# The written-out loop over the entries of an attention and gated-MLP kernel, with all steps in another program order

## The chip, the cores and the metric

The kernel runs on one core of a Trainium2 chip. The metric is device time in microseconds (us) for one whole execution: 393.02 us before the change, the median of 3 runs (392.91 to 393.31). All times below are in us. PE is the matmul engine (TensorE), PEld its weight loads, DVE the vector engine, ACT the scalar engine, POOL GpSimd, and SP the engine on whose queue nearly all DMAs are issued.

## The reference

For each of 8 batch entries with 8 heads, 576 positions and head width 64, 32 packed queries `p` attend to `k` and `v`; the result serves as keys and values for `q`; the 512-wide rows that come out pass through a gated MLP.

```python
p_packed = sm_attn(p, k, v)              # softmax(0.125 * p k^T) v
out      = sm_attn(q, p_packed, p_packed)
x = out.transpose(0, 2, 1, 3).reshape(B, S, H * D)       # 8 x 576 x 512
h = np.maximum(x @ w_in, 0.0)                            # 1024 wide
u, v = h[..., :512], h[..., 512:]
v_n = (v - mean(v)) / sqrt(var(v) + 1e-6)
v_s = einsum('ts,bsd->btd', w_spatial, v_n) + b_spatial[None, :, None]
result = (u * v_s) @ w_out
```

## The kernel before

**Arithmetic.** Each large product is made of operands split into a high and a low part, and three matmuls stand for one: high by high, high by low, low by high. The high part is a cast (on ACT mostly), the low part a subtraction (`rest`, line 82, on DVE or POOL). The spatial product and the product with `w_out` are cut in 2 by 2 blocks and done with seven block products each (`gate_product`, line 800, and `product`, line 991). Their operands are blocks, or sums of blocks, of the gated rows: g11, g12, g21, g22 and T1 to T4 (`block_sum`, line 952, on DVE; `block_hi` 977; `block_lo` 987), and of the weights: A11, A12, A22, S1 to S4. Entry 0 has its own, plainer product while the weights are still being prepared, and it is also there that A22, S1 to S4 are split.

**PSUM.** Matmul results go to four quarters of PSUM; `on(i)` (line 74) hands out quarter i, a tile `ps0` to `ps3` of two halves, once all readers of what stood there are done. So a matmul into a quarter waits for the slowest engine that still reads the quarter's old content. In before the quarters are names q0 to q3, renamed at each entry's end.

**Steps of an entry.** `value` (634) makes the v half of h, in three groups of chunks; ACT takes the relu out of PSUM; DVE and POOL work out mean and inverse deviation; ACT applies them (`norm_act`, 735). `up` (869) makes the u half in four blocks. `gate_product` 1 to 7 and `gate_add`, `gate_mult` (856, 861) make the gated blocks in the tile `u`, `product` makes the result. Between them run the attention of the next entry (its packed result `pp`, line 485, and that result's transpose `ppT`, 503; the mixed columns, copied by `mix_keep`, 602; query maxima, exponentials and sums) and the packed attention of the one after (its maxima, `nmax`).

**Order.** PE, DVE, ACT and POOL each run their instructions in the order in which the program names them: the wrapper `InOrder` (line 35) pins every call, which is why every row of the profile has its line, 43. An instruction that waits holds back all that stands behind it on its engine, and nothing else. SP's DMAs are placed by the framework. Entry 0 is written out, entry 1 too (`b = 1`, 1388), entries 2 to 4 are one loop body (1571), entries 5, 6 and 7 are written out again (1746, 1909, 2066).

Of the kernel before, what the change touches and what calls it, by code (L numbers as in the profile page):

```python
# [22 lines left out]
FH = DF // 2  # L23
# [26 lines left out]
def body(ctx: ExitStack, tc, q, k, v, vt, p, w_in, w_sp, b_sp, w_out, out):  # L50
# [1001 lines left out]

# [22 lines left out]
    load_spatial()  # L1075
    att.pack_scores(by_turns(3, 2))
    conv_v1 = to_f32(w_in_sb[:, 2:4, FH:], raw_v1, two, "vr")
    next(conv_v0)
    next(conv_v0)
    att.pack_max(0)  # L1080
    keep_warm(1, 4)
    att.pack_max(1)
    att.pack_exp(0)
    att.pack_exp(1)
    att.pack_turn(on(0), on(3)())
# [75 lines left out]
    ff.value(1, None, (1,), (1,))
    spatial_hi(2)
    ff.value(1, None, (0,), (2,))
    ff.stats(0, (1,))
    load_q(1)
    spatial_rest(3, on(0))
    ff.relu(1, (0,))
    att.query_tail(1)
    spatial_lo(4)
    ff.inverse(0, (0,))  # L1170
    ff.stats(1, (0,))
    ff.value(1, None, (1,), (2,))
    ff.inverse(0, (1,))
    next(bias)
    spatial_lo(3)
    spatial_rest(2, on(3))
    ff.relu(1, (1,))
    ff.norm(0, (0,))
    ff.inverse(1, (0,))
    conv_u1 = to_f32(w_in_sb[:, 2:4, :FH], raw_u1, one, "p1T")  # L1180
    ff.stats(1, (1,))
    ff.norm_hi(0, (0,))
    ff.value(2, on(0))
    spatial_lo(2)
    ff.norm(0, (1,))
    ff.inverse(1, (1,))
    ff.norm(1, (0,))
    ff.norm_hi(0, (1,))
    ff.gate((0,), "hm", (0,), on(2))
    ff.relu(2)  # L1190
    ff.gate((2,), "hm", (0, 1), on(1))
    tail_diff = tail_difference(pool)
    next(tail_diff)
    ff.norm_hi(1, (0,))
    ff.relu_tail()
    next(conv_u0)
    ff.gate((1,), "hm", (0,), on(3))
    ff.gate((0,), "hm", (1,))
    ff.norm(1, (1,))
    ff.gate((1,), "hm", (1,))  # L1200
    ff.norm_lo(1, (0,), pool)
    ff.gate((0,), "hm", (2,))
    ff.stats(2)
    ff.norm_hi(1, (1,))
    ff.gate((3,), "hm", (0, 1), on(0))
    next(conv_u1)
    ff.norm_lo(1, (1,), dve)
    ff.inverse(2)
    ff.gate((0,), "hm", (3,))
    ff.norm_lo(0, (0,), dve)  # L1210
    next(out01)
    ff.gate((1,), "hm", (2,))
    ff.norm_lo(0, (1,), dve)
    ff.gate((3,), "hm", (2, 3))
    out23 = prepare_out(1, raw23)
    next(out23)
    ff.norm(2)
    next(conv_u0)
    ff.gate((1,), "hm", (3,))
    ff.norm_hi(2)  # L1220
    ff.gate((1,), "l", (0, 1))
    ff.gate((0,), "l", (0, 1))
    ff.tail_hi(act.copy)
    ff.norm_lo(2)
    ff.gate((0,), "l", (2, 3))
    next(tail_diff)
    next(conv_u1)
    ff.gate((1,), "l", (2, 3))
    next(tail_diff)
    ff.gate((1,), "t")  # L1230
    ff.gate((0,), "t")
    ff.gate_keep(1, act)
    ff.gate((3,), "l", (0, 1))
    ff.gate_keep(0, act)
    ff.gate((3,), "l", (2, 3))
    nxt.pack_scores(by_turns(2, 3))
    load_k(2)
# [333 lines left out]
    for b in (2, 3, 4):  # L1571
# [135 lines left out]
        if b + 4 < B:  # L1707
            load_k(b + 4)
# [533 lines left out]
```

## Time and profile before

| what | us |
|---|---|
| median of 3 runs | 393.02 |
| span of the profiled execution, first to last instruction | 391.2 |
| median less this span | 1.8 |
| PE busy | 376.8 |
| DVE busy | 326.5 |
| ACT busy | 280.3 |
| POOL busy | 153.5 |

Busy time is the union of an engine's instructions. An entry in the middle of the kernel takes 43.9 us. Tiles carry the names of the program without their numbers: `ps_t` is any quarter of PSUM, `u` the gated rows or their blocks, `o` a spare block for c1 (the sum of gate products 1 and 2), `g_h` and `g_l` the parts of a block, `t` a part of a T sum, `wout_h` and `wout_l` parts of the last weights, `v_h` and `v_l` of the normalized rows, `a_h`, `a_l` and `m_h`, `m_l` of the attention's weights and mixed columns, `kept` the mixed columns' copy, `vr` the v half.

### The profile page before, as it was taken

To read this page: it belongs to the slowest core of one execution; us is meant where nothing else is said; L and a number is where in the kernel's file an instruction comes from. 1 tells how busy PE (TensorE), PEld (TensorE's weight loads), DVE (VectorE), ACT (ScalarE), POOL (GpSimd) and SP (SyncE) were. 2 spreads that over 40 slices of the span, in tenths; PEclk is the share of its full clock that TensorE was granted. 3 is DMA by queue.
4 is the path that set the end of the run, shared out by engine and by line. 5 is a ranking of instruction groups with operands and counts; after the bars stand their busy time and mean duration, and the time that the engine had idled before them with its cause. 6 is when DMAs were issued, how large, how long until landed. Compare 5 with 4: busy or idle time off the path is not lost.

```text
span 391.2 us, 8947 instructions
## 1 busy us (share of the span) xinstructions
PE 376.8 (96%) x3674; PEld 337.8 (86%) x3674; DVE 326.5 (83%) x502; ACT 280.3 (72%) x494; POOL 153.5 (39%) x190
## 2 busy tenths in 40 slices
PE   6889999999999999999999999999899999999995
PEld 5668978799798898998899898998699889999995
DVE  2898989995799959997799959997599969997784
ACT  3588876978975598766985598666895589558642
POOL 3467647899461040702143040703153043504120
PEclk9899999999999999999999999999999999999999
DMA  7999149630510803045300803033000600002003
GB/s 302 416 391 368 68 137 361 252 111 12 185 69 0 335 29 131 0 164 201 116 10 0 331 34 124 0 122 121 4 1 2 241 3 2 0 34 89 2 0 122
DMA packets 17660, 47.79 MB, mean 122 GB/s; under 512 B 1362, under 2 KB 11602, under 8 KB 14804
## 3 DMA queue, kind: packets, MB, share of 16 engines
q1 hardware_dynamic: 17332, 47.02, 32.3%
q8 instruction: 29, 0.48, 0.5%
q10 hardware_dynamic: 288, 0.21, 0.2%
q14 instruction: 11, 0.09, 0.1%
HBM read 37.79 MB, written 9.44 MB: 121 GB/s over the span
## 4 chain that ended last, share of the span: by engine, by line
PE 77%; DVE 10%; ACT 6%; POOL 3%; DMA 2%; issue 1%; SPq 0%; DVEq 0%; ACTq 0%
PE ps_t L43 77%; DMA kT<-in_k 2%; DVE u L43 2%; DVE o L43 1%; ACT vr L43 1%; DVE bn L43 1%; POOL bits L43 1%; DVE vr L43 1%; DVE sm_t L43 1%; POOL sm_t L43 1%; POOL rstd L43 1%; DVE v_l L43 1%; DVE m_l L43 1%; DVE sm L43 1%; ACT sm_t L43 0%
## 5 line engine op out<-in xcount | busy, mean ns | idle before, releaser
L43 POOL TENSOR_TENSOR u<-o,u 128x576 f32<-128x576 f32 x14 | 24.1, 1722 | 71.1 <-DVE o L43 70.6
L43 PE MATMUL ps_t<-t,wout_h 128*128 128x288 f32 x232 | 50.2, 300 | 0.1
L43 POOL TENSOR_TENSOR rstd<-mv,eps 128x2 f32<-128x2 f32 (+2 forms) x26 | 5.8, 222 | 107.2 <-DVE mv L43 107.2
L43 PE MATMUL ps_t<-wb_h,v_h 128*128 128x288 f32 x144 | 40.7, 300 | 0.5 <-ACT kept L43 0.3
L43 PEld LDWEIGHTS ps_t<-t,wout_h 128*128 128x128 f32 x232 | 37.8, 188 | 3.0 <-DVE t L43 2.4
L43 PE MATMUL ps_t<-wb_l,v_h 128*128 128x288 f32 x144 | 39.9, 295 | 0.0
L43 PE MATMUL ps_t<-a_h,m_h 128*128 128x288 f32 x128 | 38.6, 301 | 1.1 <-ACT ppT L43 1.1
L43 DVE TENSOR_TENSOR v_l<-vr,v_h 128x512 fp32r<-128x512 f32 x45 | 31.7, 727 | 7.9 <-ACT v_h L43 7.9
L43 PE MATMUL ps_t<-a_l,m_h 128*128 128x288 f32 x128 | 37.8, 295 | 0.0
L43 PE MATMUL ps_t<-a_h,m_l 128*128 128x288 f32 x128 | 37.8, 295 | 0.0
L43 PE MATMUL ps_t<-t,wout_l 128*128 128x288 f32 x116 | 32.4, 295 | 0.0
L43 PEld LDWEIGHTS ps_t<-wb_h,v_h 128*128 128x128 f32 x144 | 27.0, 188 | 5.1 <-issue 1.4
L43 PE MATMUL ps_t<-g_h,wout_h 128*128 128x288 f32 x104 | 29.2, 296 | 0.9 <-ACT pp L43 0.9
L43 PE MATMUL ps_t<-wsums,v_h 128*128 128x288 f32 x168 | 29.3, 296 | 0.0
L43 PE MATMUL ps_t<-g_h,wout_l 128*128 128x288 f32 x104 | 29.1, 295 | 0.0
L43 ACT CAST v_h<-vr 128x512 fp32r<-128x512 f32 x46 | 27.3, 624 | 2.3 <-DVE vr L43 1.6
L43 PE MATMUL ps_t<-wb_h,v_l 128*128 128x288 f32 x144 | 28.5, 294 | 0.0
L43 PEld LDWEIGHTS ps_t<-wb_l,v_h 128*128 128x128 f32 x144 | 27.1, 188 | 0.0
L43 PE MATMUL ps_t<-m_h,a_h 128*128 128x512 f32 x80 | 26.0, 392 | 0.1
L43 PEld LDWEIGHTS ps_t<-a_h,m_h 128*128 128x128 f32 x128 | 24.0, 188 | 2.3 <-ACT ppT L43 1.3
L43 DVE BATCH_NORM_STATS2 bn<-vr 128x6 f32<-128x512 f32 x32 | 21.1, 681 | 5.7 <-ACT vr L43 5.7
L43 PE MATMUL ps_t<-m_l,a_h 128*128 128x512 f32 x80 | 25.9, 390 | 0.0
(178 smaller groups left out, 1188.4 us busy)
## 6 DMA issues: line engine op xcount, KB each, us to landing
v_sb<-in_v SPq DMA_DIRECT2D x8, 1024.0 KB, 6.6
kT<-in_k SPq DMA_DIRECT2D x7, 1152.0 KB, 5.1
qT<-in_q SPq DMA_DIRECT2D x7, 1152.0 KB, 5.1
out_t<-prod SPq DMA_DIRECT2D x27, 288.0 KB, 2.4
raw<-in_w_in SPq DMA_DIRECT2D x4, 1024.0 KB, 9.4
raw<-in_w_out SPq DMA_DIRECT2D x2, 1024.0 KB, 7.9
kT<-in_k SPq DMA_DIRECT2D x2, 576.0 KB, 7.1
qT<-in_q SPq DMA_DIRECT2D x2, 576.0 KB, 12.4
```

The costliest lines, as they stand in the source:

```text
L43: return lambda *a, **k: self.tc.keep_in_program_order(call(*a, **k))
```

## The change

The eight entries become objects A0 to A7 (attention) and F0 to F7 (MLP), the loop over entries 2 to 4 goes, every step is a call of its own, and quarters are plain numbers. The steps, their engines and the number of instructions are the same; the order in which the calls stand is another nearly everywhere, and entries 2 to 4 no longer have one common order. The queue of SP changes little. Cut to the places that are spoken of:

```diff
-    att, nxt, far, further = (Attention(b) for b in range(4))
+    A0, A1, A2, A3, A4, A5, A6, A7 = (Attention(b) for b in range(B))
     keep_warm(1, 11)
...
     keep_warm(1, 4)
-    att.pack_max(1)
-    att.pack_exp(0)
-    att.pack_exp(1)
-    att.pack_turn(on(0), on(3)())
+    A0.pack_scores(by_turns(3, 2))
...
     out_lo(A12, pool)
...
+    F0.block_lo("g12", pool)
+    out_lo(A22, pool)
+    A1.query_sub(0, pool)
+    A3.pack_scores(by_turns(1, 2))
...
+    A2.pack_values(on(3))
...
+    A1.mix(0, on(0))
...
+    A2.packed(act)
...
+    F0.product(A11, "g11", psum=on(3), to="o11")
...
-    sum_out(S4, dve)
-    out_lo(A22, pool)
...
-    for b in (2, 3, 4):
-        att, nxt, far = nxt, far, further
-        further = Attention(b + 3)
-        ff = FeedForward(b, att, nxt)
...
-    b = 5
...
-    ff.value(0, psum=on(q1), rs=(0,))
-    ff.value(2, psum=on(q0), rs=(0,))
-    ff.value(0, rs=(1,))
-    ff.value(2, rs=(1,))
...
+    F5.value(0, psum=on(0), rs=(0,))
+    F5.value(0, rs=(1,))
+    F5.value(2, psum=on(1), rs=(0,))
+    F5.relu(0)
+    F5.value(2, rs=(1,))
...
+    F5.up_relu(1)
+    A6.packed_turned(act)
...
+    F5.norm_act(1)
...
+    F6.block_hi("g21")
+    F6.block_lo("g21")
+    F6.block_sum("T3")
+    F6.block_sum("T1")
+    F6.block_hi("T3")
```

Three places in the order follow. The number behind a name tells tiles of one name apart and differs between the kernels.

ACT's instructions at the end of entry 0, before: `m_h` is the mixed columns' high part, `a21` a block of the weights, `sm_t` the exponentials of entry 1's queries, `nmax` entry 3's packed maxima, `pp` the packed result of entry 2, read out of quarter 3.

```order
L43 CAST m_h_839<-ps0_t_841 128x1024
L43 CAST g_h_894<-u_577 128x576
L43 CAST a21_898<-bits_631 128x512
L43 ACTIVATE sm_t_851<-sm_t_851 128x576
L43 CAST g_h_894<-u_577 128x576
L43 ACTIVATE sm_t_804<-sm_t_804 128x576
L43 ACTIVATE pp_979<-ps3_t_924,rtot_727 128x64 x2
```

The same place after:

```order
L43 CAST g_h_959<-u_575 128x576
L43 CAST m_h_860<-ps0_t_862 128x1024
L43 CAST g_h_959<-u_575 128x576
L43 ACTIVATE pp_978<-ps3_t_918,rtot_734 128x64 x2
L43 ACTIVATE nmax_894<-nmax_894 128x1
L43 ACTIVATE sm_t_826<-sm_t_826 128x576
L43 ACTIVATE sm_t_807<-sm_t_807 128x576
```

The two rows of `pp` have moved ahead of both exponentials and of the cast of `a21`. On POOL, meanwhile, the low part of A22 (128x512) has moved from after the product into the row between g12's low part (`t`) and the subtraction `sm_t`, both of which stand ahead of g11's low part.

ACT's instructions in entry 5 between the relu of the value group 1 and `ppT`, before:

```order
L43 ACTIVATE vr_3552<-ps3_t_3514 128x1024
L43 COPY p1T_3572<-ps2_t_3538 128x2x4x128
L43 ACTIVATE vr_3510<-vr_3510,off_3576,rstd_3512 128x512 x2
L43 COPY p1T_3572<-ps1_t_3499 128x128
L43 CAST v_h_3489<-vr_3510 128x512
L43 ACTIVATE vr_tail_3527<-vr_tail_3527,off_3601,rstd_3529 64x512
L43 ACTIVATE vr_3552<-vr_3552,off_3611,rstd_3554 128x512 x2
L43 ACTIVATE u_3642<-ps0_t_3559 128x576
L43 COPY ppT_3645<-ps1_t_3499 128x128
```

The same place after:

```order
L43 ACTIVATE vr_3563<-ps3_t_3526 128x1024
L43 COPY p1T_3574<-ps2_t_3539 128x2x4x128
L43 ACTIVATE vr_3507<-vr_3507,off_3571,rstd_3509 128x512 x2
L43 ACTIVATE vr_tail_3513<-vr_tail_3513,off_3583,rstd_3515 64x512
L43 ACTIVATE u_3587<-ps0_t_3550 128x576
L43 COPY p1T_3574<-ps1_t_3504 128x128
L43 ACTIVATE u_3587<-ps3_t_3590 128x576
L43 COPY ppT_3604<-ps1_t_3504 128x128
```

The cast `v_h` and the two halves of `norm_act(1)` no longer stand ahead of `ppT`; the relu of a second block of u now does.

DVE's instructions in entry 6 at the end of the gating, before; `o` here is T3 (the difference g22 less g12), the second `u` is T1, `t` a low part of T3:

```order
L43 TENSOR_TENSOR u_4132<-ps3_t_4234,u_4132 128x2x288
L43 TENSOR_TENSOR o_4270<-u_4132 128x576
L43 TENSOR_TENSOR g_l_4318<-u_4132,g_h_4317 128x576
L43 TENSOR_TENSOR u_4132<-u_4132 128x2x288
L43 TENSOR_TENSOR t_4414<-o_4270,t_4414 128x576
```

The same place after:

```order
L43 TENSOR_TENSOR u_4134<-ps3_t_4232,u_4134 128x2x288
L43 TENSOR_TENSOR g_l_4318<-u_4134,g_h_4317 128x576
L43 TENSOR_TENSOR o_4248<-u_4134 128x576
L43 TENSOR_TENSOR u_4134<-u_4134 128x2x288
L43 TENSOR_TENSOR t_4402<-o_4248,t_4402 128x576
```

The low part of g21 and the sum T3 have changed places.

Two smaller moves are not shown by rows. In entry 1 the cast of v's S3 block on ACT stood before the two copies `kept` of the mixed columns and stands behind them after. In entries 1 to 4 one of the two packed maxima (`pack_most`, a reduction on DVE) stands one place or more earlier among the low parts of v, before the gate's additions.

## Rows read from the trace of the kernel before

**Rows 1.** Part 1 of the page: busy time (share of the span), instructions.
```profile
PE 376.8 (96%) x3674; PEld 337.8 (86%) x3674; DVE 326.5 (83%) x502; ACT 280.3 (72%) x494; POOL 153.5 (39%) x190
```
**Rows 2.** Busy time by stage (columns in the first line; clock 1.00 is full).
```profile
core 0: us, PE busy (x) PEld busy (x) DVE busy (x) ACT busy (x) POOL busy (x), PEclk, DMA share, GB/s
...
168.10:212.00 43.90, 43.90 (x446) 40.48 (x446) 38.06 (x62) 32.93 (x61) 12.20 (x18) 1.00 0.30 109
...
255.90:300.10 44.20, 43.10 (x416) 39.37 (x415) 37.61 (x61) 32.39 (x55) 13.40 (x18) 1.00 0.16 55
```
**Rows 3.** PE in time: start, duration, instruction, in brackets the idle before.
```profile
70.64 1.09 PE L43 MATMUL ps_t<-w_in_sb,ppT 64*32 64x512 f32 x16
72.61 0.40 PE L43 MATMUL ps_t<-g_h,wout_h 128*128 128x288 f32 x1 [0.88 <-ACT pp L43]
...
104.32 0.40 PE L43 MATMUL ps_t<-wb_h,v_h 128*128 128x288 f32 x1 [0.33 <-ACT kept L43]
...
122.01 0.53 PE L43 MATMUL ps_t<-g_l,wout_h 128*128 128x288 f32 x2 [0.49 <-DVE g_l L43]
...
277.08 0.40 PE L43 MATMUL ps_t<-a_h,m_h 128*128 128x288 f32 x1 [1.09 <-ACT ppT L43]
277.32 0.30 PE L43 MATMUL ps_t<-a_l,m_h 128*128 128x288 f32 x1
...
299.66 0.29 PE L43 MATMUL ps_t<-t,wout_h 128*128 128x288 f32 x1
299.79 0.29 PE L43 MATMUL ps_t<-t,wout_l 128*128 128x288 f32 x1
300.09 0.67 PE L43 MATMUL ps_t<-t,wout_h 128*128 128x288 f32 x3
...
339.95 0.53 PE L43 MATMUL ps_t<-g_l,wout_h 128*128 128x288 f32 x2 [0.63 <-DVE g_l L43]
```
**Rows 4.** The chain of waits, 265 to 278 us: start, duration, what.
```profile
267.02 1.04 ACT vr L43
...
274.93 1.41 ACT vr L43 x2
...
276.88 0.16 ACT ppT L43
```
**Rows 5.** POOL and ACT in time before the stall at 72.61 us.
```profile
63.92 2.69 POOL L43 TENSOR_TENSOR wout_l<-bits,wout_h 128x512 fp32r<-128x512 f32 x2 [2.20 <-ACT wout_h L43]
66.57 1.15 POOL L43 TENSOR_TENSOR sm_t<-sm_t,mx 128x576 f32<-128x576 f32 x1
67.69 1.93 POOL L43 TENSOR_TENSOR t<-u,t 128x576 fp32r<-128x576 f32 x1
69.98 1.43 POOL L43 TENSOR_TENSOR g_l<-u,g_h 128x576 fp32r<-128x576 f32 x1 [0.36 <-ACT g_h L43]
...
72.05 0.51 ACT L43 ACTIVATE pp<-ps_t,rtot 128x64 f32<-128x64 f32 x2
```
**Rows 6.** One instruction of POOL and of DVE that start together in entry 1.
```profile
117.92 1.43 POOL L43 TENSOR_TENSOR u<-o,u 128x576 f32<-128x576 f32 x1
...
117.94 2.02 DVE L43 TENSOR_TENSOR u<-o,u 128x576 f32<-128x576 f32 x1
```
**Rows 7.** ACT in time before the stall at 104.32 us.
```profile
99.41 0.63 ACT L43 CAST v_h<-s 128x512 fp32r<-128x512 f32 x1
```
**Rows 8.** DVE in time around the stall at 339.95 us.
```profile
338.47 0.76 DVE L43 TENSOR_TENSOR o<-u 128x576 f32<-128x576 f32 x1
339.14 0.75 DVE L43 TENSOR_TENSOR g_l<-u,g_h 128x576 fp32r<-128x576 f32 x1
...
340.48 0.75 DVE L43 TENSOR_TENSOR t<-o,t 128x576 fp32r<-128x576 f32 x1
```
**Rows 9.** The start and a stretch of entry 5, columns as in rows 2.
```profile
10.00:12.00 2.00, 2.00 (x21) 1.55 (x8) 1.41 (x3) 0.39 (x1) 0.83 (x1) 0.50 1.05 438
...
283.00:288.00 5.00, 5.00 (x38) 5.00 (x39) 4.89 (x8) 4.97 (x9) 0.23 (x1) 1.00 0.00 0
```

More of the change, by code (lines that the diff above doesn't have):

```diff
@@ L1169, in body @@
[L1169 to L1188, printed above, removed]
@@ L1207, in body @@
[L1207 to L1225, printed above, removed]
+    keep_warm(3, 2)
@@ new lines, in body @@
+    A2.query_lo(0)
+    A2.query_hi(1)
+    F1.add_part("P1", A12)
+    A2.query_lo(1)
+    F1.add_part("U", A22)
+    F1.add_part("P3", S1)
+    F1.add_part("P7", S1)
+    load_k(5)
+    load_q(3)
+    A2.query_tail(0, act)
+    A2.query_tail(1, act)
+    F1.put(F1.part("P1"), 0, 0)
+    F1.put(F1.part("P7"), 1, 1)
+    F1.put(F1.part("P3"), 0, 1)
+    F1.put(F1.part("U"), 1, 0)
+    load_v(4)
+    F2 = FeedForward(2, A2, A3)
+    F2.value(0, psum=on(2), rs=(0,))
+    F2.value(0, rs=(1,))
+    F2.value(2, psum=on(0), rs=(0,))
@@ new lines, in body @@
+    A3.query_tail(0, act)
+    A3.query_tail(1, act)
+    F2.product(S1, "T1", onto=S2)
+    F2.add_part("P1", A12)
+    F2.add_part("U", A22)
+    F2.add_part("P3", S1)
+    F2.add_part("P7", S1)
+    load_k(6)
+    F2.put(F2.part("U"), 1, 0)
+    F2.put(F2.part("P3"), 0, 1)
+    load_v(5)
+    load_q(4)
+    F2.put(F2.part("P7"), 1, 1)
+    F2.put(F2.part("P1"), 0, 0)
+    F3 = FeedForward(3, A3, A4)
+    F3.value(0, psum=on(3), rs=(0,))
+    F3.value(0, rs=(1,))
+    F3.value(2, psum=on(2), rs=(0,))
@@ new lines, in body @@
+    A4.query_lo(0)
+    A4.query_turn(1)
+    A4.query_tail(0, act)
+    A4.query_hi(1)
+    F3.add_part("P3", S1)
+    A4.query_lo(1)
+    F3.add_part("P1", A12)
+    F3.add_part("U", A22)
+    F3.add_part("P7", S1)
+    F3.put(F3.part("P1"), 0, 0)
+    load_q(5)
+    F3.put(F3.part("U"), 1, 0)
+    F3.put(F3.part("P3"), 0, 1)
+    load_k(7)
+    F3.put(F3.part("P7"), 1, 1)
+    load_v(6)
+    F4 = FeedForward(4, A4, A5)
+    F4.value(0, psum=on(1), rs=(0,))
+    F4.value(0, rs=(1,))
+    A4.query_tail(1, act)
@@ new lines, in body @@
+    F5.add_part("U", A22)
+    F5.add_part("P7", S1)
+    A6.query_tail(0, act)
+    A6.query_tail(1, act)
+    F5.put(F5.part("P7"), 1, 1)
+    F5.put(F5.part("P1"), 0, 0)
+    F5.put(F5.part("P3"), 0, 1)
+    load_q(7)
+    F5.put(F5.part("U"), 1, 0)
+    F6 = FeedForward(6, A6, A7)
+    F6.value(0, psum=on(3), rs=(0,))
+    F6.value(2, psum=on(1), rs=(0,))
+    A7.packed_turn(F6.ps[2])
+    F6.value(2, rs=(1,))
+    F6.value(0, rs=(1,))
+    F6.relu(2)
+    F6.tail_add()
+    F6.tail_relu()
@@ new lines, in body @@
+    F6.relu(0)
+    A7.packed_turned(act)
+    F6.value(1, psum=on(0))
+    F6.moments(2, 0)
+    F6.mean(2, 0)
+    F6.moments(0, 1)
+    F6.inverse(2)
+    F6.offset(2)
+    F6.relu(1)
+    F6.moments(0, 0)
+    F6.mean(0, 1)
+    F6.mean(0, 0)
+    F6.inverse(0)
+    F6.norm_act(2)
+    F6.moments(1, 1)
+    F6.up(0, psum=on(3))
+    F6.up(1, psum=on(0))
+    F6.offset(0)
+    F6.up_relu(0)
+    F6.norm_hi(2)
+    F6.norm_act(0)
+    F6.up_relu(1)
+    F6.moments(1, 0)
+    F6.mean(1, 1)
+    F6.mean(1, 0)
@@ new lines, in body @@
+    F6.add_part("P1", A12)
+    A7.query_lo(0)
+    F6.product(S1, "T1", onto=S2)
+    A7.query_hi(1)
+    A7.query_tail(0, act)
+    A7.query_lo(1)
+    F6.add_part("P3", S1)
+    F6.add_part("P7", S1)
+    F6.add_part("U", A22)
+    A7.query_tail(1, act)
+    F6.put(F6.part("P3"), 0, 1)
+    F6.put(F6.part("P1"), 0, 0)
+    F6.put(F6.part("P7"), 1, 1)
+    F6.put(F6.part("U"), 1, 0)
+    F7 = FeedForward(7, A7)
+    F7.value(0, psum=on(3), rs=(0,))
+    F7.value(2, psum=on(0), rs=(0,))
+    F7.value(2, rs=(1,))
@@ new lines, in body @@
+    F7.value(0, rs=(1,))
+    F7.relu(2)
+    F7.tail_add()
+    F7.value(1, psum=on(2))
+    F7.tail_relu()
+    F7.relu(0)
+    F7.moments(2, 0)
+    F7.mean(2, 0)
+    F7.moments(0, 1)
+    F7.inverse(2)
+    F7.moments(0, 0)
+    F7.mean(0, 1)
+    F7.mean(0, 0)
+    F7.offset(2)
+    F7.relu(1)
+    F7.inverse(0)
+    F7.norm_act(2)
+    F7.moments(1, 1)
+    F7.up(0, psum=on(3))
+    F7.up(1, psum=on(2))
+    F7.up(2, psum=on(0))
+    F7.up(3, psum=on(1))
+    F7.offset(0)
+    F7.up_relu(0)
```

2218 lines of the change are left out of this document (1204 added, 1014 removed).

## The prediction, made before the changed kernel ran

> **What bounds the kernel now.** I read the busy times first. PE is busy for 376.8 of 391.2 us and DVE for 326.5 [rows 1], so PE sets the end unless it is made to wait, and 14.4 us in all is what an order could give back. The table by stage comes next, because that share is an average. In a middle entry PE is busy for all 43.90 us, DVE for 38.06 and ACT for 32.93; in entry 5 PE is idle for 1.10 us [rows 2]. So the middle entries have no idle time to give and the ends of the kernel have. The third view is PE in time: it names the stalls one by one with the engine that ended them [rows 3]. Those of 0.3 us and more after the start are 0.88 before 72.61 (ACT, `pp`), 0.33 before 104.32 (ACT, `kept`), 0.49 before 122.01 (DVE, `g_l`), 1.09 before 277.08 (ACT, `ppT`) and 0.63 before 339.95 (DVE, `g_l`).
>
> An idle figure is not yet a price. Undisturbed matmuls of this form start 0.13 us apart (299.66, 299.79) and last 0.29, so idle time begins to count 0.16 after the next start was due; and the first matmul after a stall lasts 0.40 and the next starts 0.24 behind it instead of 0.13 (277.08, 277.32) [rows 3]. A stall of idle i therefore costs i + 0.16 + 0.10 = i + 0.26. The same rows show a loss that no idle figure shows: from 299.79 to 300.09 the starts lie 0.30 apart in place of 0.13, which costs 0.16. There PE waits on the low part of a block from DVE without ever running dry. So even where PE reads as busy, DVE is nearly on the path.
>
> **The change, part by part.** Instructions and engines stay as they are, so only waits can come or go. The sum is made on the profiled execution (span 391.2) and taken off the median, 393.02; the 1.8 between them is outside the span and stays.
>
> *Start, entry 0.* Four warm-up matmuls move from among the packed maxima to a place ahead of the packed scores. The granted clock is 0.50 from 10 to 12 us, half of full speed, so that of TensorE's two levels it is the lower, 1.2 GHz, and PE spends those 2.00 us busy on 21 instructions [rows 9]. If the slow stretch went, 1.0 us of PE time would be saved; if as much were added, it would be lost. But in that window the DMA engines are busy throughout (1.05), and what they bring, the weights, feeds the first large products. I halve both ends because of that cover: 0 (-0.5 to +0.5).
>
> The Trainium skill, "TensorE: Matmul & The Clock Gate", section "What's actually happening", says that the throttled clock is the default and that activity releases it. By that rule fewer matmuls between maxima and turn lengthen the slow stretch, and the sum would be less by up to 0.5; the low clock at 10 to 12 us agrees with the rule, but no row shows what the new place does.
>
> *End of entry 0 (the stall before 72.61).* The first product into quarter 3 waits for ACT to read `pp` out of it. `pp` runs at 72.05 for 0.51 us [rows 5], and ahead of it stand two exponentials and a cast that the change puts behind it. PE's last work before the stall ends at 70.64 + 1.09 = 71.73 [rows 3]; overlapping by the usual fraction of a matmul, the product could start at about 71.45, which is 1.16 earlier. What is late next is g11's low part on POOL, since the low part of A22 now stands ahead of it. From POOL's rows [rows 5]: two weights' low parts until 63.92 + 2.69 = 66.61, `t` 1.93, A22 2.69 / 2 = 1.34, the subtraction `sm_t` 1.15, `g_l` 1.43: 72.46. The product wants it after four matmuls with high parts, at 71.45 + 4 x 0.13 = 71.98. It is 0.48 late, so the gain is 1.16 - 0.48 = 0.7. The bounds: with `t` at the 1.43 of `g_l`, which has the same shape, POOL is ready in time, +1.2; with all 576-wide pieces at 1.93 and A22 lengthened alike to 1.81, it ends at 66.61 + 3 x 1.93 + 1.81 = 74.21, that is 2.2 late, -1.1. I take the rows as they stand, +0.7.
>
> Here a pair of rows matters. DVE's multiplication at 117.94 took 2.02 us while POOL's at 117.92 took 1.43 [rows 6]; DVE's subtraction of the same 576 columns, with POOL quiet, took 0.75 [rows 8]. The change moves two sums of weights on DVE, each with two operands in SBUF, to this stretch. The Trainium skill, "SBUF — State Buffer", section "Who interferes with whom", says that a DVE instruction with two SBUF inputs contends with a GpSimd instruction that reads SBUF, and that the later one is blocked fully. The 2.02 against 0.75 agrees with it. By that rule POOL's chain would run towards its long end.
>
> *Entry 1.* The stall before 104.32 ends with ACT's copy `kept`. The S3 cast of v, 0.63 us at 99.41 [rows 7], stood ahead of it on ACT and moves behind it. That is more than the stall's 0.33 + 0.26 = 0.59, less what comes late with it; I take +0.5 (0 to +0.6). The stall before 122.01 is a DVE matter: its instructions between the end of gate product 4 and the low part are the same and in the same order, so it stays: 0 (0 to +0.5, if DVE comes to that place earlier).
>
> *Entries 2 to 4.* No idle to remove. One wait of the kind at 300.09, 0.16 us, may go in each; by the same measure a maximum on DVE that stands earlier may cost up to one reduction, 0.75 (the price of a 576-wide DVE instruction [rows 8]). I take 3 x 0.1 = +0.3 (-0.8 to +0.5): nearer to the row of 300.09, because the reduction moves among low parts that the gate wants one after another, not all at once.
>
> *Entry 5 (the stall before 277.08).* The chain of waits behind it runs from ACT's relu at 267.02 to `ppT` at 276.88 [rows 4]. Two things change. `value(0)` runs both heads in one piece, without the tail group's matmuls between, so its relu and all that follows start earlier by two to four matmuls. And ACT no longer does the two halves of `norm_act(1)`, 1.41 us in one row at 274.93 [rows 4], ahead of `ppT`. `ppT` has to come earlier by 1.09 + 0.16 = 1.25 for the stall to go wholly, less than those 1.41 and the earlier relu give, even with the relu of one more block ahead of `ppT`. So 1.09 + 0.26 = 1.35 is removed. What is late next: the low parts of v's blocks, as `norm_act(1)` is later on ACT now. DVE is busy for 4.89 of 5 us from 283 to 288 [rows 9] and can't catch up what arrives late, and I give back 0.35, about two of the hidden waits of 0.16. Net +1.0 (0 to +1.3).
>
> *Entry 6 (the stall before 339.95).* PE waits for g21's low part, done at 339.14 + 0.75 = 339.89. It changes places with T3's sum at 338.47, so it comes 0.67 earlier [rows 8], of a price of 0.63 + 0.26 = 0.89. What is late next is T3: its sum ends 0.67 later, its high part on ACT follows, and its low part, at 340.48 before, slips by some 0.15, while the product that uses it is due 0.67 earlier. Before, this product wanted the low part about 0.4 after it was done; now it lacks 0.67 + 0.15 - 0.4 = 0.4. Net 0.89 - 0.4 = +0.45 (0 to +0.9).
>
> *Entry 7.* The same exchange, without a stall of that size to remove, and an addition `add_part` ahead of a low part: -0.1 (-0.3 to +0.5).
>
> The sum: 0 + 0.7 + 0.5 + 0.3 + 1.0 + 0.45 - 0.1 = 2.85, so 393.02 - 2.85 = 390.2. The terms depend on different rows; with their bounds combined as independent errors the likeliest case's own range is 388.5 to 391.7.
>
> **The rivals.**
>
> *DVE takes PE's place.* PE leaves the stalls at 72.61, 104.32 and 277.08 earlier and stands before DVE's low parts instead. For it: 4.89 of 5 us [rows 9] and the wait at 300.09 [rows 3]. Against it: DVE has 43.90 - 38.06 = 5.84 us of idle in a middle entry [rows 2], spent in the value stage, where a shift can be caught up. Only the exchange in entry 6 remains, 393.02 - 0.45 = 392.6.
>
> *POOL and DVE in each other's way at the end of entry 0.* That stretch goes from +0.7 to -1.1, which takes 1.8 off the sum: 392.0. For it is the pair of rows at 117.92 [rows 6]; against it, that `sm_t` with two operands needed just 1.15 in the same stretch [rows 5].
>
> *Slower: a maximum on DVE ahead of the gate.* In entries 1 to 4 a packed maximum stands earlier on DVE, before low parts that a gate product needs. If these have no slack, each entry is longer by one reduction, 0.75: 4 x 0.75 = 3.0, against gains of 0.7 + 1.0 + 0.45 - 0.1 = 2.05 elsewhere: 393.02 + 3.0 - 2.05 = 394.0. It decides from the point where the low parts' slack is under a fourth of a reduction, for then the four cost more than all the rest brings. For it: the 0.30 spacing at 300.09 is a place with no slack at all [rows 3]. Against it: before the change PE is busy for 43.90 of 43.90 us [rows 2] with nearly the same reductions among the low parts.
>
> *It does nothing.* The waits that go are replaced by others of equal size: 393.0, within 0.4.
>
> **How the numbers follow.** The forecast has 0.48, and 0.04 goes to still more gain, where most terms reach their upper bounds (under 388.5). DVE in PE's place has 0.13, POOL and DVE in each other's way 0.10, the slower case 0.20, nothing 0.05. What a measurement of this kernel can tell from no change is 0.2%, 0.8 us. Faster by more than that means under 392.2: 0.48 + 0.04 + 0.10, and 0.02 of the 392.6 case, 0.64. Within: 0.11 + 0.05 = 0.16. Slower: 0.20. The range goes from 387.4, where the upper bounds of the large terms meet, to 394.2, which takes in the slower case's own 394.0; beyond it lies about half of that case and little on the other side.
>
> **What would show it right or wrong.** In the profile after, no stall over 0.3 should stand at the first product of entry 0, none with `ppT` as its releaser in entry 5, and none at g21's low part in entry 6; a short one on POOL's `g_l` should stand in the first product instead, and one on T3's `t` in entry 6. The middle entries should last 43.9 less 0.1. The prediction is wrong if these entries last 44.3 or more, if entry 5 keeps its length with its stall gone, or if the time up to the first `value` of entry 1 differs by more than 1 us from the terms for the start and the end of entry 0.

## The result, and the profile after

The changed kernel takes 390.04 us (389.80 to 390.13, 4 runs) against 393.02 for the kernel before: ratio 0.9918, 95% interval 0.9904 to 0.9932. Forecast were 390.2 and a range of 387.4 to 394.2. Measured again in five rounds on another occasion, it came to 0.9947 (0.9928 to 0.9966) of the kernel before; what can make such a difference is found below, in both kernels: places where chance decides. In the first measurement all four runs of the kernel before lay in the upper part of its spread (392.91 to 393.31, of 391.35 to 393.92 over all runs) and all four of the changed kernel in its lower group, so that the first ratio may flatter the change. The profiled execution's span is 388.1, that is 3.1 less.

Where the 3.1 come from is read from PE in time: the start of the first matmul of each stage in both traces (for the last matmul, its end).

| stretch | before | after | shorter by | forecast |
|---|---|---|---|---|
| start to entry 0's first `up` | 58.16 | 58.08 | 0.08 | 0 |
| from there to entry 1's first `value` | 27.57 | 26.71 | 0.86 | 0.7 |
| entry 1, `value` to the first gate product | 18.59 | 19.07 | -0.48 | 0.5 |
| entry 1, gate product to entry 2 | 27.58 | 26.09 | 1.49 | 0 |
| entries 2 to 4 | 131.69 | 131.69 | 0.00 | 0.3 |
| entry 5 | 44.26 | 43.06 | 1.20 | 1.0 |
| entry 6 | 41.23 | 40.97 | 0.26 | 0.45 |
| entry 7 to the last matmul | 38.06 | 38.39 | -0.33 | -0.1 |
| the rest | 4.09 | 4.07 | 0.02 | |

The sum was right to 0.25; its terms were not all so. Without the 1.49 in entry 1, for which 0 was forecast, the others come to 1.6 of the 2.85 that were forecast. Of the stages that were shown before [rows 2], these are a middle entry, entry 5 and entry 6 after, with busy times and clock in the same columns:

```profile
173.84:217.77 43.93, 43.93 (x449) 40.42 (x447) 37.74 (x62) 33.57 (x62) 12.89 (x18) 1.00 0.30 110
...
261.64:304.70 43.06, 43.05 (x416) 39.44 (x415) 37.95 (x60) 31.75 (x55) 13.67 (x18) 1.00 0.16 56
304.70:345.67 40.97, 40.97 (x327) 37.12 (x326) 37.29 (x59) 29.72 (x50) 14.27 (x18) 1.00 0.09 30
```

The middle entry lasts as long as before and PE is busy throughout; entry 5 now is like it, with no idle time on PE. PE's stalls after 37 us, where the five of [rows 3] stood, are these in the trace after (start, duration, instruction, in brackets the idle time and what ended it):

```profile
58.08 0.40 PE L43 MATMUL ps_t<-a_h,m_h 128*128 128x288 f32 x1 [0.18 <-DVE m_l L43]
69.58 1.37 PE L43 MATMUL ps_t<-v_sb,p1T 128*32 128x64 f32 x80 [0.47 <-DVE u L43]
...
102.44 1.09 PE L43 MATMUL ps_t<-w_in_sb,ppT 64*32 64x512 f32 x16 [0.27 <-ACT pp L43]
103.86 0.40 PE L43 MATMUL ps_t<-wb_h,v_h 128*128 128x288 f32 x1 [0.33 <-ACT kept L43]
...
374.48 0.53 PE L43 MATMUL ps_t<-g_l,wout_h 128*128 128x288 f32 x2 [0.35 <-DVE g_l L43]
```

The stalls before 72.61, 122.01, 277.08 and 339.95 have no counterpart. The one on `kept` before 104.32 is there with the same 0.33, and three short ones are new, at 58.08, 69.58 and 102.44. The one at 374.48 stood before at 377.64, with 0.28. In entry 5 ACT shows why (before, `ppT` stood at 276.88 and started the PE's work at 277.08 [rows 3, 4]):

```profile
272.20 0.64 ACT L43 ACTIVATE u<-ps_t 128x576 f32<-128x576 f32 x1
272.73 0.25 ACT L43 COPY p1T<-ps_t 128x128 f32<-128x128 f32 x1
272.88 0.65 ACT L43 ACTIVATE u<-ps_t 128x576 f32<-128x576 f32 x1
273.42 0.26 ACT L43 COPY ppT<-ps_t 128x128 f32<-128x128 f32 x1
...
274.61 1.54 ACT L43 ACTIVATE vr<-vr,off,rstd 128x512 f32<-128x512 f32 x2
```

Counted from the entry's first `value` (261.64 in this trace, 263.59 before), `ppT` is done after 12.04 instead of 13.44: 1.40 earlier, little more than the 1.25 that the stall asked for. `norm_act(1)` follows it.

In entry 1 the pair of multiplications that [rows 6] show has another outcome. DVE, then POOL, in the trace after:

```profile
117.44 0.79 DVE L43 TENSOR_TENSOR u<-o,u 128x576 f32<-128x576 f32 x1
...
117.70 1.83 POOL L43 TENSOR_TENSOR u<-o,u 128x576 f32<-128x576 f32 x1
```

Before, POOL began 0.02 ahead and took 1.43, and DVE took 2.02. Now DVE begins 0.26 ahead and takes 0.79, and POOL 1.83. The low part that ended the stall before 122.01 comes 1.2 earlier relative to the gate product, and that stretch of entry 1 is the largest single gain.

### The profile page after: what moved, and what is told of

It is laid out like the page before. It is cut to its first block, busy times and chain, and to the rows that moved or that the text cites. A ratio compares the mean times of both kernels' runs of the same rounds, so it can differ in the third digit from the quotient of the medians.

```text
span 388.1 us, 8952 instructions
## 1 busy us (share of the span) xinstructions
PE 375.9 (97%) x3674; PEld 336.2 (87%) x3674; DVE 325.6 (84%) x502; ACT 281.1 (72%) x494; POOL 156.4 (40%) x190
## 4 chain that ended last, share of the span: by engine, by line
PE 85%; DVE 4%; ACT 4%; POOL 3%; DMA 2%; issue 1%; SPq 0%; DVEq 0%; ACTq 0%
PE ps_t L43 85%; DMA kT<-in_k 2%; DVE u L43 1%; POOL bits L43 1%; POOL rstd L43 1%; DVE sm_t L43 1%; DVE bits L43 1%; DVE mx L43 1%; ACT p1T L43 1%; ACT p L43 0%; POOL off L43 0%; DVE o L43 0%; ACT vr L43 0%; POOL wsums L43 0%; DVE bn L43 0%
## 5 line engine op out<-in xcount | busy, mean ns | idle before, releaser
L43 DVE TENSOR_TENSOR v_l<-vr,v_h 128x512 fp32r<-128x512 f32 x45 | 33.6, 761 | 6.9 <-ACT v_h L43 6.6
L43 POOL TENSOR_TENSOR sm_t<-sm_t,mx 128x576 f32<-128x576 f32 x15 | 23.2, 1559 | 8.0 <-DVE mx L43 7.8
L43 ACT CAST g_h<-u 128x576 fp32r<-128x576 f32 x24 | 16.1, 671 | 13.9 <-DVE u L43 11.8
```

The lines of the kernel that those rows point to most:

```text
L43: return lambda *a, **k: self.tc.keep_in_program_order(call(*a, **k))
```

## The experiments

All runs are of one core, and each is compared with the kernel before on the same chip.

**Entry 5, both moves, and one of them.** The edit of the run e5_both, in which the first pair of lines is `value` and the second ACT's order; the run e5_ppT has the second part alone.

```diff
     ff.value(0, psum=on(q1), rs=(0,))
-    ff.value(2, psum=on(q0), rs=(0,))
     ff.value(0, rs=(1,))
+    ff.value(2, psum=on(q0), rs=(0,))
...
-    ff.norm_act(1)
     ff.up(2, psum=on(q0))
     ff.up_relu(0)
-    ff.v_sum("S1")
     nxt.packed_turned(act)
+    ff.norm_act(1)
+    ff.v_sum("S1")
```

> The kernel before with two moves in entry 5 alone: value(0) in one piece, and ppT with the relu of one block of u ahead of norm_act(1) on ACT. Theory (the ACT chain in front of ppT is the price of the stall before 277.08): the stall is gone, its 1.35 less what DVE gives back, so 392.0 (391.7 to 392.2). Rival (DVE takes PE's place from 277 to 300): the stall goes, the entry keeps its 44.3 us, 392.8 to 393.2.

> The kernel before, with ppT and one relu ahead of norm_act(1) in entry 5 alone, value(0) as before. Theory (ACT's 1.41 us of norm_act(1) is the larger part of the stall before 277.08): the entry gets shorter by 1.0 to 1.3, the kernel takes 392.0. Rival (the relu of value(0) matters as much): 0.3 to 0.6, 392.5.

Measured: e5_both 391.27, ratio 0.9966 (0.9951 to 0.9980); e5_ppT 391.20, ratio 0.9969 (0.9955 to 0.9983). Entry 5 lasts 42.97 in the one and 42.99 in the other, against 44.26: 1.29 and 1.27 shorter. So ACT's order alone makes the gain, `value(0)` in one piece adds 0.02 (the entry itself scatters by 0.08, 44.23 to 44.31, in the profiles that leave it unchanged), and DVE gives back 0.08 of the 1.35 that the stall cost, not the 0.35 that was set aside. ACT in e5_ppT:

```profile
274.81 0.64 ACT L43 ACTIVATE u<-ps_t 128x576 f32<-128x576 f32 x1
275.34 0.26 ACT L43 COPY ppT<-ps_t 128x128 f32<-128x128 f32 x1
275.49 1.53 ACT L43 ACTIVATE vr<-vr,off,rstd 128x512 f32<-128x512 f32 x2
```

In the listing in time `ppT` stood at 276.77 before; at 275.34, with 0.26 for the copy, it is just early enough, as PE's matmul that waits for it was due at about 275.8.

**The pair of multiplications in entry 1, first try.** Ten small writes were put on POOL to make it late.

```diff
+    idle = const.tile([P, 32], F32, name="idle")
...
+    for _ in range(10):
+        pool.memset(idle, 0.0)
     ff.gate_mult("g22", "c7", pool)
```

> The kernel before, with ten small writes by POOL (128x32, to a tile that nothing reads) ahead of its multiplication of g22 in entry 1, so that DVE's multiplication of g21 starts first. Theory (the 2.02 us of DVE's multiplication at 117.94 is a block by POOL's, which started 0.02 us earlier): DVE's multiplication takes 0.8, the stall before 122.01 goes, entry 1 is about 1.2 us shorter from its first product to the next value stage, and the kernel takes 391.8. Rival (that stretch is shorter in the changed kernel because of its other order on DVE): the multiplication keeps about 2 us or the stage keeps its 12.85 us, and the kernel takes 392.9 to 393.3.

Measured: 393.21, ratio 1.0004 (0.9991 to 1.0016). That is the rival's time, but it decides nothing, as the trace shows that the experiment missed its aim. DVE, then POOL:

```profile
115.55 2.39 DVE L43 TENSOR_TENSOR m_l<-kept,m_h 128x1024 fp32r<-128x1024 f32 x1
...
118.76 1.81 DVE L43 TENSOR_TENSOR u<-o,u 128x576 f32<-128x576 f32 x1
...
115.42 1.44 POOL L43 TENSOR_TENSOR o<-extra,o 128x576 f32<-128x576 f32 x1 [1.08 <-ACT extra L43]
116.80 1.76 POOL L43 MEMSET idle<- 128x32 f32 x10
118.52 1.44 POOL L43 TENSOR_TENSOR u<-o,u 128x576 f32<-128x576 f32 x1
```

POOL's addition began 0.13 ahead of DVE's subtraction `m_l`, which then took 2.39 instead of 1.22; so DVE came late to its multiplication too, and POOL was ahead again, by 0.24. Two blocks in place of one. And chance had a part in it: ahead of both, at 107.98, PE waited 0.24 for a DMA (`kT`, the keys of the packed scores), which it does not do in the kernel before, and all that follows in the entry came later by about 0.25.

**The pair, second try.** POOL's multiplication of g22 in entry 1 is left out.

```diff
     ff.gate_mult("g21", "U")
-    ff.gate_mult("g22", "c7", pool)
```

> The kernel before, leaving out POOL's multiplication of g22 in entry 1 (entry 1's result is another for that). Theory (POOL's multiplication blocks DVE's): DVE's multiplication of g21 takes 0.8, the stretch from entry 1's first product to the next value stage takes 11.4 to 11.7 instead of 12.85, and the kernel takes 391.9 (391.6 to 392.4). Rival (order of DVE's other steps): that stretch keeps 12.5 or more, 392.8 to 393.3.

Measured: 392.33, ratio 0.9989 (0.9975 to 1.0003), so by time alone it can't be told from no change. DVE's multiplication takes 0.79 (at 118.62), and from the first product to the next value stage it is 11.61, as the theory has it. The median falls by 0.5 and not by the 1.2 of the block. Two things in the traces can explain that: the kernel before doesn't always meet the block, and the profiled run lost 0.47 before its first product, to the wait for `kT`:

```profile
108.91 0.48 PE L43 MATMUL ps_t<-kT,pT 64*32 64x288 f32 x8 [0.44 <-DMA kT<-in_k]
```

Both show in the other runs that contain entry 1 of the kernel before unchanged. The two starts, DVE's duration and two stretches of entry 1:

| run | POOL starts | DVE starts | DVE takes | gate to first product | first product to next `value` |
|---|---|---|---|---|---|
| before | 117.92 | 117.94 | 2.02 | 14.73 | 12.85 |
| e5_both | 117.38 | 117.39 | 2.02 | 14.72 | 12.84 |
| e5_ppT | 117.71 | 117.72 | 2.02 | 14.73 | 12.89 |
| e0_pp_max | 120.68 | 120.69 | 2.03 | 15.44 | 12.86 |
| e0_all | 122.19 | 122.20 | 2.02 | 14.73 | 12.83 |
| e0_pp | 120.35 | 120.34 | 0.76 | 14.72 | 11.59 |
| e0_all_m | 120.20 | 120.16 | 0.76 | 14.73 | 11.57 |
| e6_swap | 118.64 | 118.35 | 0.83 | 15.17 | 11.65 |

This is the pair in e0_pp, where DVE is first by 0.01 (DVE, then POOL):

```profile
120.34 0.76 DVE L43 TENSOR_TENSOR u<-o,u 128x576 f32<-128x576 f32 x1
...
120.35 2.05 POOL L43 TENSOR_TENSOR u<-o,u 128x576 f32<-128x576 f32 x1
```

One hundredth of a us decides 1.25 us. Five of these eight profiles have the long stretch and three the short one, depending on a start that differs from run to run. The longer way to the first product, in e0_pp_max and e6_swap, is the wait for `kT` again (0.68 and 0.38 idle). The runs of the kernel before spread from 391.35 to 393.92; both chances fit that in size, but single runs were not traced for it.

**The changed kernel again.**

> The changed kernel once more, in five rounds. If its gain is in the order alone, it stands at 390.0 (389.7 to 390.4), and its runs lie closer together than those of the kernel before, which went from 391.9 to 393.8, since in entry 1 its two multiplications of DVE and POOL start 0.26 us apart. If the gain were luck of the first measurement, the ratio would come out at 0.995 or more.

Measured: 389.92, ratio 0.9947 (0.9928 to 0.9966), four runs from 389.63 to 390.06 and two of 391.23 and 391.41. The gain holds, but the expectation that its runs lie close together does not. In this profile DVE is first in entry 1 by 0.25 (117.17 against 117.42), as in the first; what may lengthen some runs is shown by the next kernel.

**Two moves on the changed kernel.**

```diff
-    F1.v_hi("A12")
     A2.mix_keep(1)
     F1.gate_product(1, psum=on(2))
     A2.mix_keep(0)
+    F1.v_hi("A12")
...
-    F7.block_sum("T3")
     F7.block_hi("g21")
+    F7.block_lo("g21")
+    F7.block_sum("T3")
     F7.block_hi("T3")
     F7.keep_part("P1", A11)
-    F7.block_lo("g21")
```

> The changed kernel with two moves: in entry 1 ACT's cast of v's A12 block behind the two copies of the mixed columns, in entry 7 the low part of g21 ahead of the sum T3 on DVE. Theory (ACT is the limit before entry 1's gate, and its copy holds the first gate product): the gate starts 0.5 earlier, at 103.35, and the stretch from there keeps its length; entry 7's end gets 0.1 to 0.3 shorter, as in entry 6; 389.3 (388.9 to 389.7). Rival (DVE's low part of A12, later by the same time, holds gate product 2; T3 takes the place of g21 as in the swap alone): 389.8 to 390.2.

Measured: 391.28, ratio to the kernel before 0.9956 (0.9939 to 0.9974), no better than the changed kernel. Its runs fall in two groups, three of 389.46 to 389.97 and seven of 391.19 to 391.98, and the profile is of the second (391.32). Entry 1's gate does start earlier, 18.69 after `value` instead of 19.07, but the low part of A12 then comes late by the same time and entry 1 lasts 45.13 against 45.16. In entry 7 the swap brings nothing (12.26 from the first product to the last matmul, 12.19 without). The rival was right in both. But the profile caught something else, in entry 2: from the gate to the first product it takes 15.05 where the changed kernel takes 13.49. DVE's low parts `v_l`, `m_l` and `g_l` and POOL's second subtraction `sm_t` there, here:

```profile
156.08 0.68 DVE L43 TENSOR_TENSOR v_l<-vr,v_h 128x512 fp32r<-128x512 f32 x1
156.68 1.22 DVE L43 TENSOR_TENSOR m_l<-kept,m_h 128x1024 fp32r<-128x1024 f32 x1
157.82 0.75 DVE L43 TENSOR_TENSOR g_l<-u,g_h 128x576 fp32r<-128x576 f32 x1
...
156.24 3.35 POOL L43 TENSOR_TENSOR sm_t<-sm_t,mx 128x576 f32<-128x576 f32 x1
```

and in the changed kernel:

```profile
156.60 0.68 DVE L43 TENSOR_TENSOR v_l<-vr,v_h 128x512 fp32r<-128x512 f32 x1
157.20 2.18 DVE L43 TENSOR_TENSOR m_l<-kept,m_h 128x1024 fp32r<-128x1024 f32 x1
...
156.76 1.54 POOL L43 TENSOR_TENSOR sm_t<-sm_t,mx 128x576 f32<-128x576 f32 x1
```

It is the same contest with the other loser. In both traces POOL's subtraction starts 0.16 behind DVE's `v_l` and ends well after it. In the changed kernel it runs next and `m_l` waits; here `m_l` and `g_l` run first, although POOL's start lies 0.44 ahead of that of `m_l`, and POOL takes 3.35. The exponentials come late by 1.8, and PE stands idle for 1.43. So the changed kernel has one such place less in entry 1, where DVE was first in all four profiles of its order, and one more in entry 2, where one of the four went the long way. That this is what made two of the runs of the changed kernel 1.4 longer fits in size, but no profile fell on such a run of that kernel.

**The pair in entry 7.** The kernel with the two moves, and five small writes on POOL ahead of its multiplication in entry 7.

```diff
+    for _ in range(5):
+        pool.memset(idle, 0.0)
     F7.gate_mult("g22", "c7", pool)
```

> The same, with five small writes by POOL ahead of its multiplication of g22 in entry 7, so that DVE's multiplication of g21 starts first. Theory (POOL's multiplication, at 370.06, blocks DVE's at 370.82 by 0.5): DVE's multiplication takes 0.8 instead of 1.27, all of DVE's steps behind it come 0.5 earlier, and the kernel ends 0.2 to 0.5 earlier than without the writes: 388.9. Rival (PE has the end of entry 7, or T3's sum then waits for g22): no difference to the run without the writes, within 0.2.

Measured: 390.73, ratio 0.9952 (0.9936 to 0.9968). From the first product to the last matmul it takes 12.94, which is 0.68 longer than without the writes. DVE, then POOL:

```profile
370.72 1.98 DVE L43 TENSOR_TENSOR u<-o,u 128x576 f32<-128x576 f32 x1
...
369.83 0.86 POOL L43 MEMSET idle<- 128x32 f32 x5
370.65 1.44 POOL L43 TENSOR_TENSOR u<-o,u 128x576 f32<-128x576 f32 x1
```

The five writes were not long enough, and POOL began 0.07 ahead of DVE, the worst case seen in this entry. (Entry 2 went the short way in this profile, 13.49, which fits the lower median.) With POOL 0.76 ahead (370.06, the changed kernel) DVE takes 1.27, with 0.07 it takes 1.98, and behind DVE it costs DVE nothing. The theory of the block stands; as a repair this failed.

**Entry 6, the swap alone.**

```diff
-    ff.block_sum("T3")
     ff.block_lo("g21")
+    ff.block_sum("T3")
```

> The kernel before, with the low part of g21 ahead of the sum T3 on DVE in entry 6. Theory (the term of the sum: 0.89 gained at g21, 0.4 lost at T3): 392.6 (392.4 to 392.8), with the stall before 339.95 gone and one of 0.2 to 0.4 at T3's low part. Rival (T3 is on the path as it is, so that the swap only moves the wait): 393.0, within 0.15.

Measured: 392.86, ratio 0.9997 (0.9985 to 1.0009), and entry 6 lasts 41.23, as before. The rival was right. PE in that run, where the stall before 339.95 had been [rows 3]:

```profile
339.36 0.43 PE L43 MATMUL ps_t<-g_l,wout_h 128*128 128x288 f32 x2
339.83 0.40 PE L43 MATMUL ps_t<-t,wout_h 128*128 128x288 f32 x1
340.07 0.30 PE L43 MATMUL ps_t<-t,wout_l 128*128 128x288 f32 x1
340.21 0.29 PE L43 MATMUL ps_t<-t,wout_h 128*128 128x288 f32 x1
340.34 0.29 PE L43 MATMUL ps_t<-t,wout_l 128*128 128x288 f32 x1
340.63 0.66 PE L43 MATMUL ps_t<-t,wout_h 128*128 128x288 f32 x3
```

The idle time is gone, but the first matmul with T3 starts 0.2 late, the first with its low part 0.15 late, and more of the same follows at 345. No figure of idle time shows any of it; the distance of the starts does.

**The end of entry 0, one step after the other.** The run e0_pp moves only `pp` ahead of a21's cast and the exponentials on ACT:

```diff
     far.pack_values(on(3))
+    far.packed(act)
+    out_hi(A21)
+    nxt.query_exp(1)
     ff.block_hi("g22")
     ff.block_lo("g11", pool)
     nxt.query_exp(0)
     nxt.query_add(1)
     nxt.mix(0, on(0))
-    far.packed(act)
```

(the two lines of a21 and the exponential stood above `pack_values`). The run e0_pp_max also moves entry 3's maxima and first exponential up, e0_all also one product on PE and two steps on POOL, e0_all_m also g21's cast and one low part:

```diff
+    further.pack_most(0)
+    further.pack_most(1)
     far.packed(act)
+    further.pack_scale(0, act)
     nxt.query_exp(1)
+    further.pack_exp(0)
...
     ff.product(A12, "g22", onto="o12", to="o12")
+    ff.product(A21, "g12", psum=on(2), to="o22")
...
     ff.block_lo("g22", pool)
+    out_lo(A21, pool)
+    nxt.query_norm(1, pool)
...
+    ff.block_hi("g21")
     far.packed(act)
...
     nxt.mix_hi(0)
+    nxt.mix_lo(0)
```

> The kernel before, with the two rows of pp on ACT ahead of the cast of a21 and both exponentials at the end of entry 0; POOL's order stays. Theory (pp alone holds the first product): the product starts about 1.0 us earlier, at 71.6, and the kernel takes 392.1 (391.9 to 392.4). Rival (the exponentials, now later on ACT, hold entry 1's attention back, or entry 1's ACT-bound stretch takes the gain): the product starts earlier but the kernel takes 392.7 to 393.2.

> The kernel before, with pp ahead on ACT at the end of entry 0, and with entry 3's packed maxima ahead of the sums on DVE and the first of its exponentials ahead of g22's and a21's casts and of one query exponential on ACT, as in the changed kernel; POOL's order stays. Theory (the second product waits for quarter 1, which the exponential of entry 3's scores frees, so that pp helps only together with it): no stall of 1.97, the product stage of entry 0 keeps its 13.1, and the kernel takes 392.1 (391.8 to 392.4). Rival (whatever is put first, ACT is the limit there): the stage gets longer by 1 or more, and the kernel takes 393 to 394.5.

> The kernel before, with the order of the changed kernel at the end of entry 0 on all four engines but for A22's place on POOL: pp, maxima and exponentials as in the run before (e0_pp_max), the two products with A12 ahead of the one with A21 into quarter 2 on PE, and g21's and g22's low parts ahead of a21's on POOL. Theory (pp's gain is kept only if the products that follow wait for nothing, which takes PE's and POOL's order too): no stall in that stage, the next value stage starts at 84.8 instead of 85.7, and the kernel takes 392.0 (391.7 to 392.4). Rival (the gain at that end came from what the changed kernel does before 58 us): the value stage starts at 85.5 or later, 392.7 to 393.5.

> The run before it (e0_all), with two more steps put as in the changed kernel: ACT's cast of g21 ahead of pp (ACT waits there for 1.05), and the low part of the mixed columns' second half, which frees quarter 0, ahead of the query steps that wait for POOL on DVE. Theory (each product of this stage waits for one release: pp, the two exponentials, the low part m_l, and g21's low part; only the whole set gains): no stall over 0.2 in the stage, the next value stage starts at 84.6 to 85.1, 0.6 to 1.1 earlier than in the kernel before, and the kernel takes 392.1 (391.8 to 392.5). Rival (the cause lies in the steps before 69 us, which this order doesn't change): again another wait of 0.5 or more, 393 to 395.

Measured, with the times from entry 0's first `up` to its first product and from there to entry 1's `value`:

| run | us | ratio (95%) | up to product | product to `value` |
|---|---|---|---|---|
| before | 392.75 to 393.06 | 1 | 14.45 | 13.12 |
| e0_pp | 394.72 | 1.0043 (1.0027 to 1.0058) | 13.51 | 16.52 |
| e0_pp_max | 395.30 | 1.0077 (1.0059 to 1.0094) | 13.49 | 15.85 |
| e0_all | 397.63 | 1.0123 (1.0102 to 1.0144) | 13.52 | 18.59 |
| e0_all_m | 394.14 | 1.0040 (1.0026 to 1.0055) | 13.49 | 16.74 |
| changed kernel | 390.04 | 0.9918 (0.9904 to 0.9932) | 13.72 | 12.99 |

Every one of the four brings the first product 0.95 forward, as the theory has it, and every one then loses 2.7 to 5.5. All four came out on the slower side, and the theory was wrong each time. Of the rivals' times only that of e0_all_m was met (394.14, in 393 to 395); the other three kernels were slower than either case. In e0_pp, e0_all and e0_all_m some 1.4 to 1.5 of the loss is not a stall but the lower clock behind it (last section). PE's largest stall in each, in the order of the table:

```profile
75.47 0.40 PE L43 MATMUL ps_t<-t,wout_h 128*128 128x288 f32 x1 [1.97 <-ACT p L43]
```
```profile
76.47 1.88 PE L43 MATMUL ps_t<-t,a 128*128 128x288 f32 x12 [1.40 <-ACT p L43]
```
```profile
83.64 0.86 PE L43 MATMUL ps_t<-g_h,a 128*128 128x288 f32 x4 [1.97 <-DVE m_l L43]
```
```profile
83.32 0.40 PE L43 MATMUL ps_t<-g_h,wout_l 128*128 128x288 f32 x1 [2.28 <-POOL wout_l L43]
```

Each step removes the stall that the run before had shown and meets the next: the first exponential (quarter 1), the second (quarter 2), the low part `m_l` (quarter 0), and last the low part of A22 on POOL. In e0_all_m the products run without a wait from 71.15 to 81 and then stand for that last one: A22's split, which is behind the attention's low part `a_l` in POOL's order, and which the changed kernel has ahead of the product. POOL in e0_all_m, then in the changed kernel:

```profile
79.86 1.73 POOL L43 TENSOR_TENSOR a_l<-extra,a_h 128x576 fp32r<-128x576 f32 x1 [2.09 <-ACT a_h L43]
81.55 1.72 POOL L43 TENSOR_TENSOR wout_l<-bits,wout_h 128x512 fp32r<-128x512 f32 x1
...
68.20 1.80 POOL L43 TENSOR_TENSOR wout_l<-bits,wout_h 128x512 fp32r<-128x512 f32 x1
```

That it would have been the last piece was not tried. Nor have the four kernels the changed kernel's order in all else: there, A21 by g12 (quarter 2) stands behind A22 by g21 on PE, in e0_all and e0_all_m ahead of A21 by g11. What keeps the gain at this end as a whole is not shown.

## Why the prediction was right, point by point

*Start.* 0 was taken, 0.08 measured, which is less than this time scatters (57.66 to 58.63 in the ten profiles with the start of the kernel before, 57.59 to 58.08 in the four with the changed one); the first gate product of entry 0 is 0.35 later and this is made good by 58 us. The granted clock is low at another place than in [rows 9]: 0.72 from 12 to 16 us and 0.86 from 16 to 20, 1.00 from 8 to 12. By 58 us none of this can be seen any more. The Trainium skill, "TensorE: Matmul & The Clock Gate", section "What's actually happening", was drawn on for a loss of up to 0.5 here; the measurement does not bear it out. The slow stretch moved but did not grow: the mean granted clock from 8 to 20 us is 0.86 in both traces.

*End of entry 0.* The size was right, 0.7 against 0.86 (against 0.63, if the 12.89 from product to `value` is taken that the five other profiles with the order of the kernel before show, instead of this trace's 13.12), and the step behind it half wrong. `pp` no longer holds the product, as said. But the price was put on POOL's `g_l` (0.48 late). POOL was done with it at 72.49, as worked out (72.46), and the wait is only 0.12, the gap before 72.55, because the product itself came 0.35 later than said, at 71.80: another stall came, 0.47 on DVE's `u` at 69.58, which frees quarter 3 for `pack_values`. The step that failed is "the low part of A22 ahead of g11's low part" as a mere cost. In e0_all_m, where it stands late, it is a stall of 2.28, so its place belongs to what keeps the gain; and with `pp` alone, in e0_pp, the products that follow stall for longer (1.97) than the one that was freed (0.88).

*Entry 1.* The sum 0.5 against 1.01, from two terms that were wrong in opposite ways. The cast of S3 behind `kept` was to remove the stall before 104.32, +0.5; it came out as -0.48. ACT's normalization of the first chunks (`vr`) there starts at 96.69 instead of 95.90, after a wait for POOL's `off`, and from then on ACT works without a pause up to the copy; 0.48 of the 0.94 by which PE came earlier were lost in that. ACT before, then after:

```profile
95.90 1.50 ACT L43 ACTIVATE vr<-vr,off,rstd 128x512 f32<-128x512 f32 x2
...
96.69 1.52 ACT L43 ACTIVATE vr<-vr,off,rstd 128x512 f32<-128x512 f32 x2 [0.31 <-POOL off L43]
```

Then "the stall before 122.01 stays, 0": it went, and 1.49 with it. The instructions on DVE are the same and in the same order, which is what the step was argued from; but the 2.02 of one of them was a block by POOL, whose own order and arrival had changed. The prediction had that pair before its eyes and used it for the end of entry 0 only. That the sum came out all the same is luck: this gain, which was not forecast and which depends on a block that five of eight profiles met, stands in for what other terms fell short.

The Trainium skill, "SBUF — State Buffer", section "Who interferes with whom", says that a DVE instruction with two SBUF inputs contends with a GpSimd instruction that reads SBUF, that the shared ports are an exclusive lock, and that the order of issue decides who waits. The pairs of multiplications shown here agree: the later one ends not much under its own length after the earlier one (before, DVE 0.61 after POOL's end, for 0.75 alone; in e0_pp, POOL 1.30 after DVE's end, for 1.43). Entry 2 of after_e1_e7 does not: there POOL's subtraction, by its start in the trace 0.44 ahead of `m_l`, waited for `m_l` and for `g_l` too. Where POOL already waits and DVE has several such instructions in a row, either engine can be next. The rival that rested on it was placed at the wrong end of the kernel and with the wrong sign.

*Entries 2 to 4.* +0.3 was taken, 0.00 measured. Waits of the kind that was to go are still there: in entry 4, matmuls start 0.29 apart at 254.14, as at one place in each of these entries before. The slower rival, a maximum ahead of the gate, did not come about: the entries are as long as before to 0.03, each 43.9 and not the 43.8 that was named as a sign.

*Entry 5.* Right, with its mechanism: 1.0 against 1.20, and 1.27 for ACT's order alone. The margin was as thin as it was worked out, 1.40 for the 1.25 needed. Mis-sized were the part of `value(0)`, which is 0.02, and what DVE gives back, which is 0.08 for 0.35.

*Entry 6.* +0.45 was taken for the exchange of g21's low part and T3. In the changed kernel the entry is 0.26 shorter, but the exchange alone brings 0.00: the term failed, since T3's high part and low part take the whole of it, with matmuls that start late, not with idle time. The 0.26 come from other moves in that entry, which were not taken apart.

*Entry 7.* -0.1 against -0.33, within the term's bounds; the stall on `g_l` stays, 0.35 at 374.48 for 0.28 before.

DVE in PE's place, the first rival, holds for two terms, entry 6 and (with ACT) the gate of entry 1, and not for entry 5. "It does nothing" is excluded by both measurements.

*Sums.* The bounds of the terms, added as independent errors, give 389.0 to 392.7 and not the 388.5 to 391.7 that the prediction names for its likeliest case; entry 6's 0.89 - 0.4 is 0.49, not 0.45; and four reductions cost more than 2.05 once the slack is under a third of one, not a fourth. None of this moves the forecast of 390.2.

## What to carry to other kernels

Price a stall by what stands behind it, too: an engine that is let go earlier meets the next release, and one step of a reordering taken alone can cost several times what the whole set gains at that place (a net 2.5 against 0.9 here). Read durations before orders: an instruction of DVE that takes 2.0 where its like takes 0.75 is a wait in disguise, and a neighbour on POOL that starts at nearly the same time decides it (from 0.76 ahead it still cost 0.5 here), so leave a margin between such pairs or put one of the two elsewhere. Where two such starts lie closer than the runs scatter, the kernel has more than one length, and one profile shows one of them.

## What the runs showed of the hardware beyond that

Behind the three longest of the stalls shown, two of 1.97 and one of 2.28, PE's clock fell to its lower level. In e0_pp, behind the stall of 1.97 (columns as in the tables by stage: the clock is the third number from the end):

```profile
75.40:80.00 4.60, 4.53 (x22) 4.54 (x23) 4.57 (x7) 3.75 (x9) 4.28 (x4) 0.63 0.44 175
```

and in e0_all_m, some time behind the stall of 2.28:

```profile
85.00:88.00 3.00, 3.00 (x14) 3.00 (x14) 2.09 (x3) 0.97 (x3) 2.84 (x3) 0.50 0.27 98
```

At a granted clock of 0.50 (1.2 of the 2.4 GHz) matmuls of 288 columns start 0.24 apart instead of 0.13, and the 13 starts from 85.02 to 87.89 in e0_all_m cost another 1.4 on top of the stall. In e0_all, behind its stall of 1.97, the clock is 0.50 from 84.50 to 87.60 too. Behind the stall of 1.40 in e0_pp_max and behind the stalls of 0.88 and 1.09 of the kernel before the clock stayed at 1.00. And ten writes of 128x32 by POOL took 1.76, 0.18 each, where writes of 128x1 at the kernel's start begin 0.03 apart (those go to different tiles, the ten all to one, and which of the two makes the difference was not tried); the five writes in entry 7 were sized by the 1.76, and took 0.86.
